# Four copies of the row of k's maxima, and a spread read that takes them by quarters of the partitions

## The chip, the cores and the metric

One core of one Trainium2 chip runs the whole program in one launch. The metric is the device time of an execution in microseconds (us). The engines are TensorE (PE, its weight loads PEld), VectorE (DVE), ScalarE (ACT), GpSimd (POOL) and SyncE (SP), which here issues every transfer.

## What is computed

Eight batches, eight heads, 576 tokens, head size 64: linear attention, then a gated layer with a causal convolution of five taps as gate.

```python
q_s = softmax(q, axis=-1)                 # over the 64 channels of a head
k_s = softmax(k, axis=2)                  # over the 576 tokens
kv = np.einsum('bhsd,bhse->bhde', k_s, v)
x = np.einsum('bhsd,bhde->bhse', q_s, kv) # then heads side by side: (8, 576, 512)
gate = sigmoid(sum(conv_w[t] * x shifted by 4 - t tokens))
out = (gate * (x @ w_val)) @ w_out
```

Softmax over k's tokens needs, for each of the 512 columns (head and channel), the maximum over 576 tokens. This maximum, its way into a tile, is what the change is about.

## The kernel before, in words

Each batch is a unit of work. Its tokens stand in five parts of up to 128 (four full, and a tail of 64 that two batches share); its 512 channels in four blocks of 128. For a batch, TensorE forms kv from the exponentials of k and from v (line 407), turns q (439), multiplies the turned q with kv to x (attend, 487), and makes two products with the weights, value and project (534), each in three passes, since operands are split in a high and a low part. DVE, ACT and POOL do the softmaxes, the convolution (taps: `tap` on DVE, `far` on ACT with `near` on POOL), the splits and the copies out of PSUM.

The order is written out by hand: the list ORDER names every step, and each engine takes its instructions from the list in that order. The engines wait for each other through semaphores alone. SyncE has one queue: a DMA that waits holds back all behind it. Batches are staggered: k of batch 3 is prepared while batch 1 goes through the products.

For batches 2 to 7 the maxima of k go this way:

- `load_km b j` (line 281) loads a copy of k with the channels on partitions: partition p holds the channels 4p to 4p+3, one j at a time. `k_peak b j` (286) reduces it on DVE over the tokens to one column of the tile `kpk`, [128, 4].
- `k_row b` (288 to 291) writes `kpk` to a row of 512 numbers in DRAM, `krow`: 16 bytes from each partition, side by side.
- `k_spread b` (293 to 296) reads this one row of 2 KB into every one of the 128 partitions of the tile `kmax`, [128, 512]. It waits on SyncE until `k_row` has landed. `kmax` has a single buffer, so a batch's spread also waits until the batch before has been subtracted.
- `k_sub b i` (298 to 301) subtracts `kmax` from the five parts of k, most on POOL, some on DVE; `k_exp` and `kt_exp` (305, 309) take exponentials on ACT, and `kv` uses them.

Other steps that are spoken of: `load_q` (209, 211), whose tile `q_max` (361) reduces on DVE; `load_k` (199), 1 MB; `load_kt` (204), the tails of k of two batches; `load_v` (215); `copy b n` (through line 171 on ACT or 173 on DVE) from PSUM into one of the two buffers `o`; and `put b n` (577), the store of such a block to the output. In the list, `k_spread 2` has `put 0 0`, `load_km 3 0` and `load_q 3` after it on SyncE; `k_spread 3` has `put 0 3` right after it.

Of the kernel before, what the change touches and what calls it, by code (L numbers as in the profile page):

```python
# [7 lines left out]
F32 = mybir.dt.float32  # L8
# [9 lines left out]
C = H * D  # L18
P = 128
NB = C // P  # L20
MAIN = 4 * P
TAPS = 5
HALF = S // 2
KM = 3
F32_BATCHES = (0, 1)
EPS = 1e-9
MOST = 122880 - 2.0 ** -7
# [119 lines left out]
def gated_linear_attention(ctx: ExitStack, tc: tile.TileContext, q, k, v, qt, kt, vt, kc, km, w_val, w_out, ident_in, out):  # L147
    nc = tc.nc
# [5 lines left out]
    rowpool = ctx.enter_context(tc.tile_pool(name="rowpool", bufs=1, space=bass.MemoryType.DRAM))  # L154
# [5 lines left out]
    def block(tag, name, bufs, dtype=F32, n=S):  # L160
        return work.tile([P, S], dtype, tag=tag, name=name, bufs=bufs)[:, :n]
# [13 lines left out]
    def times(e, out, in_, factor):  # L175
        if e == "a":
            nc.scalar.mul(out, in_, factor)
        elif e == "p":
            nc.gpsimd.tensor_scalar(out, in_, factor, 1.0, op0=ALU.mult, op1=ALU.mult)
        else:  # L180
            nc.vector.tensor_scalar_mul(out, in_, factor)

    T = {}
# [54 lines left out]
    def part(i, e="a"):  # L238

        lo = T["words", i][:, :, 0].bitcast(U32)  # L240
        f = T["f", i] = block("f", f"f{i}", KM, I32, lo.shape[1])
        times(e, f, lo, 2.0 ** -29)
# [35 lines left out]
    def load_km(b, j):  # L278

        t = T["km", b, j] = block("f", f"km_{b}_{j}", KM)  # L280
        nc.sync.dma_start(out=t, in_=km[b, j])
# [5 lines left out]

    def k_row(b):

        t = T["krow", b] = rowpool.tile([C], F32, tag=f"krow{b}", name=f"krow{b}")  # L290
        nc.sync.dma_start(out=t.rearrange("(p j) -> p j", j=NB), in_=T["kpk", b])

    def k_spread(b):

        t = T["kmax", b] = small.tile([P, C], F32, tag="kmax", name=f"kmax_{b}", bufs=1)
        nc.sync.dma_start(out=t, in_=T["krow", b].rearrange("(o n) -> o n", o=1).broadcast_to([P, C]))

    def k_sub(b, i, e="p", h="a"):
        mx, cs = T["kmax", b], cols(h)
# [141 lines left out]
    def q_across(b):  # L441
        if ("qT", b) not in T:
            T["qT", b] = work.tile([P, NB, S], F32 if b in F32_BATCHES else F32R, tag="qT", name=f"qT_{b}")
        return T["qT", b]
# [31 lines left out]
    def attend(b, p):  # L476

        T["x", b, p] = halved_bank(f"x_{b}_{p}")
        qh = T["qT", b][:, p]
        if b in F32_BATCHES:  # L480
            parts = ((kvd[b % 2][:, p], qh),)
# [161 lines left out]
```

## Time and profile before

| | |
|---|---|
| median of 3 runs | 304.78 us (304.15 to 305.87) |
| the profiled execution | 305.72 us, of which the span is 303.9 |
| k_row (`krow<-kpk`), 6 issues | 2.0 KB each, median 3.5 us from issue to landing |
| k_spread (`kmax<-krow`), 6 issues | 256.0 KB each, median 4.0 us |
| k tails (`kt<-in_k_tail`), 3 issues | 256.0 KB each, median 2.9 us |
| DMA packets of the run | 17454, 51.25 MB |

The span runs from the first to the last instruction; the 1.8 us more of the execution lie around it. In rows of instructions the first number is the start in us from the span's start, the second the duration. In rows of groups the three numbers behind the colon are the shortest, the median and the longest duration in ns. The row "DMA to landing" gives the same three, in us, from a DMA's issue to its landing. A bracket at a row's end tells how long the engine was idle before it, and what ended that.

### The profile page before, as it was taken

To read this page: it belongs to the slowest core of one execution; us is meant where nothing else is said; L and a number is where in the kernel's file an instruction comes from. 1 tells how busy PE (TensorE), PEld (TensorE's weight loads), DVE (VectorE), ACT (ScalarE), POOL (GpSimd) and SP (SyncE) were. 2 spreads that over 40 slices of the span, in tenths; PEclk is the share of its full clock that TensorE was granted. 3 is DMA by queue.
4 is the path that set the end of the run, shared out by engine and by line. 5 is a ranking of instruction groups with operands and counts; after the bars stand their busy time and mean duration, and the time that the engine had idled before them with its cause. 6 is when DMAs were issued, how large, how long until landed. Compare 5 with 4: busy or idle time off the path is not lost.

```text
span 303.9 us, 6467 instructions
## 1 busy us (share of the span) xinstructions
PE 279.1 (92%) x2536; PEld 271.1 (89%) x2536; DVE 255.5 (84%) x350; ACT 216.2 (71%) x357; POOL 220.4 (73%) x206
## 2 busy tenths in 40 slices
PE   0347899999999899999999999999999999999995
PEld 0336699999989799999999999999998999999995
DVE  3999999999999798999999898999779876836611
ACT  3999999967795996869673964659496885464220
POOL 4677959799989699659787879784886949752500
PEclk9978999999999999999999999999999999999999
DMA  7999491389598822618597099023201210021012
GB/s 240 408 405 396 156 397 45 103 187 361 194 319 261 327 102 75 217 54 284 158 395 304 39 259 332 17 90 106 38 0 39 80 41 0 2 116 41 0 62 96
DMA packets 17454, 51.25 MB, mean 169 GB/s; under 512 B 2705, under 2 KB 3089, under 8 KB 14737
## 3 DMA queue, kind: packets, MB, share of 16 engines
q1 hardware_dynamic: 17424, 50.85, 47.9%
q8 instruction: 20, 0.33, 0.5%
q14 instruction: 10, 0.07, 0.1%
HBM read 41.39 MB, written 9.45 MB: 167 GB/s over the span
## 4 chain that ended last, share of the span: by engine, by line
PE 66%; ACT 11%; DVE 10%; DMA 7%; issue 2%; POOL 2%; SPq 1%; ACTq 0%; DVEq 0%
PE out L534 26%; PE val L534 25%; PE x L487 7%; PE kv L407 4%; PE qTps L439 3%; DVE qs L377 3%; DMA q<-in_q 3%; DMA words<-in_w_val 2%; ACT q L392 2%; DMA out<-o 2%; DVE qm L361 1%; ACT L523 1%; DVE qs L378 1%; ACT qT L171 1%; DVE gate L511 1%
## 5 line engine op out<-in xcount | busy, mean ns | idle before, releaser
L534 PE MATMUL val<-x,w_val_hi 128*128 128x288 f32 x512 | 88.4, 294 | 0.0
L534 PEld LDWEIGHTS val<-x,w_val_hi 128*128 128x128 f32 x512 | 74.8, 188 | 0.0
L511 DVE SCALAR_TENSOR_TENSOR gate<-x,cw,gate 128x573 f32<-128x573 f32 (+3 forms) x91 | 72.1, 807 | 2.2 <-ACT gate L500 1.2
L520 POOL TENSOR_TENSOR gate<-gate,far 128x572 f32<-128x572 f32 (+3 forms) x37 | 49.5, 1341 | 27.3 <-ACT far L516 26.4
L534 PE MATMUL out<-gh,w_out_lo 128*128 128x288 f32 x256 | 55.9, 297 | 1.1 <-ACT o L171 0.6
L534 PE MATMUL val<-x,w_val_lo 128*128 128x288 f32 x256 | 56.0, 299 | 0.0
L534 PE MATMUL out<-gh,w_out_hi 128*128 128x288 f32 x256 | 55.0, 294 | 0.0
L534 PEld LDWEIGHTS out<-gh,w_out_lo 128*128 128x128 f32 x256 | 41.2, 188 | 2.1 <-ACT o L171 0.9
L534 PEld LDWEIGHTS val<-x,w_val_lo 128*128 128x128 f32 x256 | 40.7, 188 | 0.7 <-DVE x L173 0.2
L534 PEld LDWEIGHTS out<-gh,w_out_hi 128*128 128x128 f32 x256 | 41.2, 188 | 0.0
L560 POOL TENSOR_TENSOR gl<-g,gh 128x576 fp32r<-128x576 f32 x24 | 34.6, 1449 | 7.2 <-ACT gh L171 5.0
L534 PE MATMUL out<-gl,w_out_hi 128*128 128x288 f32 x256 | 39.2, 294 | 0.0
L516 ACT ACTIVATE far<-x,cw 128x572 f32<-128x572 f32 (+3 forms) x37 | 27.0, 745 | 13.7 <-DVE gate L511 6.7
L534 PEld LDWEIGHTS out<-gl,w_out_hi 128*128 128x128 f32 x256 | 35.7, 188 | 0.0
L552 DVE TENSOR_TENSOR g<-val,gate 128x576 f32<-128x576 f32 x32 | 24.0, 751 | 10.0 <-PE val L534 5.8
L366 POOL TENSOR_TENSOR q<-q,qm 128x512 f32<-128x512 f32 x29 | 31.0, 1086 | 0.7 <-issue 0.7
L171 ACT COPY o<-out 128x576 f32<-128x576 f32 x27 | 17.2, 637 | 16.7 <-PE out L534 11.5
L301 POOL TENSOR_TENSOR k<-k,kmax 128x512 f32<-128x512 f32 x21 | 28.6, 1377 | 0.1
L506 DVE TENSOR_TENSOR x<-x,x 128x576 fp32r<-128x576 f32 x32 | 23.2, 747 | 6.3 <-ACT far L516 4.1
L523 ACT ACTIVATE gate<-gate 128x576 f32<-128x576 f32 x32 | 21.1, 685 | 8.4 <-DVE gate L511 5.4
L394 POOL TENSOR_TENSOR q<-q,qs 128x512 f32<-128x512 f32 x25 | 26.0, 1048 | 0.8 <-DVE qs L379 0.6
L500 ACT ACTIVATE gate<-x,cw 128x576 f32<-128x576 f32 x27 | 19.9, 747 | 6.8 <-PE x L487 5.2
(88 smaller groups left out, 522.1 us busy)
## 6 DMA issues: line engine op xcount, KB each, us to landing
out<-o SPq DMA_DIRECT2D x31, 288.0 KB, 2.2
v<-in_v SPq DMA_DIRECT2D x8, 1040.0 KB, 8.9
q<-in_q SPq DMA_DIRECT2D x7, 1024.0 KB, 7.7
km<-in_k_strided SPq DMA_DIRECT2D x24, 288.0 KB, 4.8
k<-in_k SPq DMA_DIRECT2D x6, 1024.0 KB, 7.9
kc<-in_k_channels SPq DMA_DIRECT2D x8, 288.0 KB, 7.6
words<-in_w_val SPq DMA_DIRECT2D x4, 517.0 KB, 6.9
words<-in_w_out SPq DMA_DIRECT2D x4, 512.0 KB, 7.7
```

The lines of the kernel that those rows point to most:

```text
L301: engine(e).tensor_sub(kk[r, cs], kk[r, cs], mx[r, cs])
L366: engine(e).tensor_tensor(qq, qq, m, op=ALU.add if b < 2 else ALU.subtract)
L394: engine(e).tensor_mul(qq, qq, s.unsqueeze(2).broadcast_to([P, H, D]))
L487: nc.tensor.matmul(T["x", b, p][:, cs], a, z[:, cs], start=(i == 0), stop=(i == len(parts) - 1))
L506: nc.vector.tensor_sub(xl, T["x", b, p], T["xh", b, p].bitcast(F32))
L511: nc.vector.scalar_tensor_tensor(out=a, in0=x, scalar=w, in1=a, op0=ALU.mult, op1=ALU.add)
L516: nc.scalar.activation(T["far", b, p, j], T["x", b, p][:, :S - n], AF.Copy, scale=cw[:, p, j:j + 1])
L520: nc.gpsimd.tensor_add(a, a, T["far", b, p, j])
L523: nc.scalar.activation(T["gate", b, p], T["gate", b, p], AF.Sigmoid)
L534: nc.tensor.matmul(ps[:, cs], a[:, kb, ms], z[:, cs], start=(i == 0), stop=(i == len(parts) - 1))
L552: nc.vector.tensor_mul(T["g", b, m], T["val", b, m], T["gate", b, m])
L560: engine(e).tensor_sub(T["gl", b, m], T["g", b, m], T["gh", b, m].bitcast(F32))
```

## The change

`krow` becomes four times as long: four copies of the row, 2 KB each, one behind the other. `k_row` is still one DMA; its source repeats each partition's four numbers four times, and its destination puts each repeat into another copy. `k_spread` is still one DMA; its source pattern is now 4 copies x 32 repeats x 512 numbers, so that partitions 0 to 31 read the first copy, 32 to 63 the second, and so on. It was 128 repeats x 512 numbers. ORDER, the buffers in SBUF and all other steps are as they were; the number of instructions on each engine and their order are unchanged.

```diff
+ROWS = 4
...
     def k_row(b):
 
-        t = T["krow", b] = rowpool.tile([C], F32, tag=f"krow{b}", name=f"krow{b}")
-        nc.sync.dma_start(out=t.rearrange("(p j) -> p j", j=NB), in_=T["kpk", b])
+        t = T["krow", b] = rowpool.tile([ROWS * C], F32, tag=f"krow{b}", name=f"krow{b}")
+        peaks = T["kpk", b].unsqueeze(1).broadcast_to([P, ROWS, NB])
+        nc.sync.dma_start(out=t.rearrange("(a p j) -> p a j", a=ROWS, j=NB), in_=peaks)
 
     def k_spread(b):
 
         t = T["kmax", b] = small.tile([P, C], F32, tag="kmax", name=f"kmax_{b}", bufs=1)
-        nc.sync.dma_start(out=t, in_=T["krow", b].rearrange("(o n) -> o n", o=1).broadcast_to([P, C]))
+        own = T["krow", b].rearrange("(a n) -> a n", a=ROWS)
+        nc.sync.dma_start(out=t, in_=own.unsqueeze(1).broadcast_to([ROWS, P // ROWS, C]))
```

## The prediction

> **What bounds the kernel now.** I read the page's totals first, then the waits of PE, then the chain of work that ended last.
>
> ```profile
> span 303.9 us, 6467 instructions
> PE 279.1 (92%) x2536; PEld 271.1 (89%) x2536; DVE 255.5 (84%) x350; ACT 216.2 (71%) x357; POOL 220.4 (73%) x206
> ```
>
> TensorE is the bound: 279.1 of 303.9 us, and most of what is left lies ahead of its first matmul. So an edit to two small DMAs matters only where it makes PE wait, or ends one of its few waits. From 30 us on PE's list of waits has six entries, each of a single wait, and none is longer than the first (who waits, for whom: us in total, times, longest):
>
> ```profile
> PE x L487 <- ACT k L171: 0.8, 1, 0.8
> ```
>
> Nothing large can be won; an added wait, on the other hand, is paid in full, since PE has almost no idle time later to give it back from. The question is therefore where the two changed DMAs stand on a chain that reaches PE. The chain of work over 60 to 110 us, in order of time (start, length, what), answers it:
>
> ```profile
> 65.09 8.03 DMA q<-in_q
> ...
> 91.73 5.04 DMA out<-o
> ...
> 104.24 3.44 PE out L534 x24
> ```
>
> Two transfers lie on it: the load of q for batch 3, and the store of one output block (put 0 3), whose buffer the copy of a later block needs. SyncE's queue shows what was issued just ahead of each:
>
> ```profile
> 62.70 0.33 SPq L296 DMA_DIRECT2D kmax<-krow  x1
> ...
> 65.09 0.47 SPq L209 DMA_DIRECT2D q<-in_q  x1
> ...
> 91.28 0.33 SPq L296 DMA_DIRECT2D kmax<-krow  x1
> 91.73 0.34 SPq L577 DMA_DIRECT2D out<-o  x1
> ```
>
> In both places it is k_spread, the very DMA that the change rewrites: for batch 2 shortly ahead of the q load (a store and a km load stand between them), for batch 3 directly ahead of the store. And both landings are waited for without slack (square brackets: idle before, and its releaser), on DVE, on ACT, and through ACT's next pieces on PE (the last row is a window: its length, then the busy us of PE, PEld, DVE, ACT and POOL):
>
> ```profile
> 73.14 2.29 DVE L361 TENSOR_REDUCE qm<-q 128x32 f32<-128x2048 f32 x1 [0.41 <-DMA q<-in_q]
> ```
>
> ```profile
> 96.85 0.64 ACT L171 COPY o<-out 128x576 f32<-128x576 f32 x1 [3.25 <-DMA out<-o]
> ```
>
> ```profile
> 102.72 0.81 PE L487 MATMUL x<-qT,kvs 128*128 128x288 f32 x4 [0.76 <-ACT o L171]
> ```
>
> ```profile
> 96.85:102.70 5.85, 5.11 (x39) 4.88 (x37) 3.92 (x4) 5.77 (x7) 3.85 (x4) 1.00 0.97 385
> ```
>
> From 96.85 to 102.7 ACT is busy for 5.77 of 5.85 us, and PE has already waited 0.76 us there. So a microsecond more on that store is a microsecond of PE.
>
> **The change, part by part.** No instruction moves: every engine's row of instructions is the same before and after, and only the two access patterns differ, six times each.
>
> *k_row* sends 512 pieces of 16 bytes where it sent 128. SyncE waits for it before it can issue k_spread, and everything behind in its queue waits too:
>
> ```profile
> SPq L296 <- DMA krow<-kpk: 17.6, 6, 4.9
> ```
>
> Its price comes from landings. The quickest k_row landed in 1.9 us (first row: minimum, median, maximum), a store of 144 KB takes 1.8 us:
>
> ```profile
> DMA to landing us min/median/max: 1.9/3.9/6.6
> ```
>
> ```profile
> out<-o SPq DMA_DIRECT2D x2, 144.0 KB, 1.8
> ```
>
> So the pieces themselves are about 0.1 us of the 1.9, the rest is fixed. Four times as many make +0.3 us; the lower bound is 0, the upper +1.9, if all of the landing grew by as much again. I take 0.3, from the nearer row, the store.
>
> *Issuing k_spread.* Its pattern gains a step. Six issues took 319 to 327 ns, those of the k load 333 to 1007 ns:
>
> ```profile
> L296 SPq DMA_DIRECT2D kmax<-krow x6: 319/326/327, 62.7 to 212.2; - x6
> ```
>
> ```profile
> L199 SPq DMA_DIRECT2D k<-in_k x6: 333/518/1007, 37.1 to 179.4; - x6
> ```
>
> The bounds are 0 and +0.7 us; I take +0.2, nearest to the k load's median.
>
> *Carrying k_spread* is the large term. The source pattern's outermost step counted 128 (all rows the same row). Now it counts 4, with 32 repeats inside. If the transfer is dealt out over the 16 DMA engines by outermost steps, there are four to deal: four engines with 64 KB each instead of sixteen with 16 KB. No transfer of this trace has fewer than 128 outermost steps, so no row shows such a case, but the price has near rows. A k load of 1024 KB also brings 64 KB to each engine, a kt load of 256 KB 16 KB. Their landings, k's first and then kt's (minimum, median, maximum):
>
> ```profile
> DMA to landing us min/median/max: 5.4/7.9/10.7
> ```
>
> ```profile
> DMA to landing us min/median/max: 2.9/2.9/8.2
> ```
>
> The quickest of each differ by 5.4 - 2.9 = 2.5 us for 48 KB more per engine. Against that stands a gain. Batch 7's spread, with nothing else in flight, took 3.8 us where kt takes 2.9:
>
> ```profile
> kmax<-krow SPq DMA_DIRECT2D x1, 256.0 KB, 3.8
> ```
>
> I read the 0.9 us as the cost of sixteen engines reading one 2 KB row; with one engine to each copy it goes. Net, a spread alone would land 2.5 - 0.9 = 1.6 us later, and four engines are held that much longer. The Trainium skill says the same in "DMA: Bandwidth & Descriptors", "Why a DMA increments its semaphore by 16 and not by 1": the number of engines is the largest up to 16 that divides the slowest step of both patterns; that would be 4 here, and it speaks against the change; no run here shows it yet. The same page's 27 GiB/s per engine makes an estimate of 1.7 us for the 48 KB where the rows give 2.5, and by it the sum below would be +0.5 us.
>
> What of the 1.6 us reaches the two transfers? Later packets on those four engines stand behind the spread, and catch up only in idle time. DMA share is the last but one column:
>
> ```profile
> 63.00:75.00 12.00, 12.00 (x87) 11.47 (x86) 11.38 (x14) 10.12 (x14) 12.00 (x12) 1.00 0.92 308
> 91.00:97.00 6.00, 6.00 (x47) 6.00 (x47) 5.89 (x8) 2.69 (x5) 5.92 (x7) 1.00 0.80 216
> ```
>
> Between the spread and the q load's landing (10 us at 0.92) 0.8 us is idle: 1.6 - 0.8 = 0.8 us later. The issue of that q load hangs on PE, not on k_row, so the first two terms don't add. For the store (6 us at 0.80) 1.2 is idle: 0.4 later, plus 0.3 and 0.2, since it is issued right after k_row's landing and k_spread's issue: 0.9 us.
>
> *Batches 4 to 7* cost nothing. The issues of batches 4 and 5 on SyncE (batch 7's, at 212.2, is the last start in the row of issues above), and the first readers of their tiles, on POOL and for batch 7 on DVE:
>
> ```profile
> 126.13 0.32 SPq L296 DMA_DIRECT2D kmax<-krow  x1
> ...
> 147.29 0.33 SPq L296 DMA_DIRECT2D kmax<-krow  x1
> ```
>
> ```profile
> 130.12 1.30 POOL L301 TENSOR_TENSOR k<-k,kmax 128x512 f32<-128x512 f32 x1
> ...
> 136.46 2.69 POOL L520 TENSOR_TENSOR gate<-gate,far 128x573 f32<-128x573 f32 x2 [3.46 <-ACT far L516]
> ...
> 155.28 1.30 POOL L301 TENSOR_TENSOR k<-k,kmax 128x512 f32<-128x512 f32 x1
> ```
>
> ```profile
> 235.15 0.91 DVE L301 TENSOR_TENSOR k<-k,kmax 128x512 f32<-128x512 f32 x1
> ```
>
> Batch 4's spread is read 4.0 us after its issue. With the three terms it comes 2.1 us later than now and may be a microsecond too late for POOL, which has 3.46 us of idle time soon behind to make it good. In batch 5 the first reader follows 8 us after the issue, in batch 7 23 us; batch 6 lies between. Without that cover each late spread would cost up to its 2.1 us.
>
> **Sum.** 0.8 (batch 2, through q) + 0.9 (batch 3, through the store) = +1.7 us. The two add, as the second follows the first on the same chain. The profiled execution took 305.7 us (303.9 of span); that makes 307.4. It lay 0.9 above the median of 304.78; on the median I forecast 306.5 us.
>
> **Rivals.**
> *Not slower: the transfer stays on 16 engines.* Only k_row's 0.3 and the issue's 0.2 are added, at batch 3. Reading four rows could take back part of the 0.9 us of the spread. That gives between -0.4 and +0.5 us: 304.4 to 305.3. For it: nothing in before shows a transfer on fewer. Against: none of its transfers has so short an outer step. It decides if the spread alone still lands within 3.8 us.
> *Faster by over 0.5%* (1.5 us, about what a measurement of this kernel can tell from no change) would need more than the one store's wait to go; of PE's waits of at most 0.8 us only the one at 102.7 has been traced back here to a DMA. It would give about 303.
> *Much slower: the row stays contended.* Four engines read four neighbouring rows, and the 0.9 us isn't won. Then the spread alone lands 2.5 us later, and of that 1.7 and 1.3 reach the two transfers, or all of it twice if the idle time doesn't help; with 0.5 at batch 3 that is +3.5 to +5.5 us, in the middle +4.5: 309.3. The busiest spread of before (5.9 us) speaks for it:
>
> ```profile
> DMA to landing us min/median/max: 3.1/4.0/5.9
> ```
>
> **Chances.** Few engines as summed 0.55, sixteen engines 0.24, contended 0.18, faster 0.03. The first case runs from +0.5 (idle time covers all but k_row and the issue) to +3.7 (it covers nothing); about six tenths of it, 0.33, are above 1.5 us. So slower 0.33 + 0.18 = 0.51, faster 0.03, the same 0.46. The range leaves out the worse half of the contended case, the lowest part of the sixteen-engine one, and faster: 304.6 to 309.3.
>
> **What would show it.** Right: batch 7's spread lands in about 5.4 us; k_row at its quickest in 2.2; DVE's wait for q at 73 grows by about 0.8, ACT's for the store at 96.8 by 0.9, and PE's at 102.7 follows. Wrong: a lone spread of 3.8 us or less, or one of 5.4 with PE's waits unchanged, which would mean that the two transfers do not queue behind it.

## The result and the profile after

The changed kernel took 309.54 us (median of 4 runs, 308.96 to 309.96) against 305.32 us before (4 runs): ratio 1.0138, 95% interval 1.0093 to 1.0184. It was measured twice more, beside more runs of before: 307.51 against 305.17 (ratio 1.0073, 1.0046 to 1.0100) and 307.70 against 305.35 (1.0078, 1.0045 to 1.0112). So it is slower by some 2.3 us in two measurements and by 4.2 us in the first; the intervals (1.4 to 3.4 us, and 2.8 to 5.6) overlap. The profiled execution of the first measurement took 309.16 us, of which the span is 307.3. In the table of experiments below, the medians of e1, e13 and e14 count one slow run each (469 to 708 us) that their ratios leave out.

First the question on which the large term rested: on how many DMA engines does the spread run? A transfer closes with a small completion packet on every engine that carried a part of it; the windows below show 16 of them, then 4. The hardware queue of before, then of after (packets, MB, share of 16 engines):

```profile
q1 hardware_dynamic: 17424, 50.85, 47.9%
```

```profile
q1 hardware_dynamic: 19656, 50.88, 47.6%
```

These are 2232 packets more. k_row alone should add 6 x 384 = 2304, one for each further piece of 16 bytes. The 72 that are missing are 6 x 12: each spread ends with 4 completions instead of 16. Batch 7's spread, alone in the queue, shows the engines themselves. Windows around it of before (212 to 217 us), of after (216 to 221 us), each with the busy share of the 16 engines in tenths and GB/s in 40 slices; the packets under 512 B are its completions:

```profile
DMA  0000000000009249968998884452000000000000
GB/s 0 0 0 0 0 0 0 0 0 0 0 0 98 16 33 115 197 197 164 213 164 147 164 164 66 147 180 99 0 0 0 0 0 0 0 0 0 0 0 0
DMA packets 145, 0.27 MB, mean 54 GB/s; under 512 B 16, under 2 KB 16, under 8 KB 144
```

```profile
DMA  0000000000002212222512212222222221000002
GB/s 0 0 0 0 0 0 0 0 0 0 0 0 49 66 66 115 98 98 98 98 66 98 82 66 82 98 98 98 98 115 115 82 115 66 16 33 16 33 16 82
DMA packets 133, 0.27 MB, mean 54 GB/s; under 512 B 4, under 2 KB 4, under 8 KB 132
...
q14 instruction: 1, 0.01, 0.4%
```

The busy share falls from eight or nine tenths to two (4 of 16 is 0.25), and the rate from about 160 to about 95 GB/s. All four completions lie within the second window; what its last slice shows is in part a packet of another queue (the row q14). So the spread's traffic ends 4.7 us after its issue (216.25), where before it ended 3.3 us after (212.23): about 1.5 us later.

Where does this reach PE? In PE's list of waits, x behind a copy by ACT now has two entries; before it had one.

```profile
PE x L490 <- ACT o L172: 2.4, 2, 1.4
```

ACT's copy that waits for put 0 3, and PE behind it, in the changed kernel:

```profile
98.97 0.64 ACT L172 COPY o<-out 128x576 f32<-128x576 f32 x1 [5.14 <-DMA out<-o]
```

```profile
99.67 0.80 PE L490 MATMUL x<-qT,kvs 128*128 128x288 f32 x4 [1.45 <-ACT o L172]
...
104.84 0.81 PE L490 MATMUL x<-qT,kvs 128*128 128x288 f32 x4 [0.94 <-ACT o L172]
```

The copy starts 2.1 us later than before (98.97 against 96.85), and so does PE's second step (104.84 against 102.72). SyncE's rows tell why:

```profile
86.16 0.38 SPq L293 DMA_DIRECT2D krow<-kpk  x1
...
91.97 0.55 SPq L299 DMA_DIRECT2D kmax<-krow  x1
92.64 0.39 SPq L580 DMA_DIRECT2D out<-o  x1
```

The store goes out at 92.64 instead of 91.73, 0.9 us later. Of this, 0.2 us is k_row's own later issue (86.16 against 85.94), 0.5 its longer landing, and 0.2 the longer issue of k_spread. The store then takes 6.26 us in the chain of work where it took 5.04, behind a spread on four engines:

```profile
92.64 6.26 DMA out<-o
```

So far PE has lost 2.1 of the 3.4 us by which the span has grown. Part of the rest is lost at a place of which the prediction said that it costs nothing. POOL, then PE, at batch 4:

```profile
133.58 1.30 POOL L304 TENSOR_TENSOR k<-k,kmax 128x512 f32<-128x512 f32 x1 [1.29 <-DMA kmax<-krow]
134.84 0.90 POOL L477 TENSOR_TENSOR qTlo<-qTt,qT 128x128 fp32r<-128x128 f32 x1
```

```profile
135.26 0.29 PE L490 MATMUL x<-qTlo,kvs 128*128 128x288 f32 x1
135.79 0.40 PE L490 MATMUL x<-qTlo,kvs 128*128 128x288 f32 x1 [0.24 <-POOL qTlo L477]
136.03 0.43 PE L537 MATMUL out<-gh,w_out_lo 128*128 128x288 f32 x2
```

The same work of PE before, the two multiplications with qTlo in one row:

```profile
133.22 0.43 PE L487 MATMUL x<-qTlo,kvs 128*128 128x288 f32 x2
133.49 0.43 PE L534 MATMUL out<-gh,w_out_lo 128*128 128x288 f32 x2
```

The instruction right behind the waiting k_sub on POOL, tail_low, makes an operand of PE's next step. POOL's idle time, at 136 us in the profile before, was to make the wait good; it comes behind this instruction, too late. The wait of 0.24 us is only what PE still shows of it: PE reaches the first of the two multiplications 2.0 us behind the profile before (135.26 against 133.22), and the product after them 2.5 us behind (136.03 against 133.49). At batch 5 the same order of steps costs another 0.4 us or so. There k_sub waits for a late load of k, and tail_low again stands behind it:

```profile
159.78 1.30 POOL L304 TENSOR_TENSOR k<-k,kmax 128x512 f32<-128x512 f32 x1 [1.93 <-DMA k<-in_k]
161.05 0.46 POOL L477 TENSOR_TENSOR qTlo<-qTt,qT 128x128 fp32r<-128x128 f32 x1
```

The last 0.4 us are lost in smaller steps after that and have not been traced.

### The profile page after: what moved, and what is told of

It reads as the page before. It is cut to its first block, busy times and chain, and to the rows that moved or that the text cites. A ratio compares the mean times of both kernels' runs of the same rounds, so it can differ in the third digit from the quotient of the medians.

```text
span 307.3 us, 6467 instructions
## 1 busy us (share of the span) xinstructions
PE 280.9 (91%) x2536; PEld 271.8 (88%) x2536; DVE 255.3 (83%) x350; ACT 216.2 (70%) x357; POOL 221.4 (72%) x206
## 4 chain that ended last, share of the span: by engine, by line
PE 51%; DVE 14%; ACT 14%; DMA 13%; issue 3%; POOL 2%; SPq 1%; ACTq 0%; POOLq 0%; DVEq 0%
PE out L537 23%; PE val L537 19%; PE x L490 5%; DMA out<-o 4%; DVE qs L380 4%; PE kv L410 3%; DVE gate L514 2%; DMA k<-in_k 2%; DMA words<-in_w_val 2%; DMA krow<-kpk 2%; ACT q L395 2%; DVE qm L364 2%; PE qTps L442 2%; ACT L526 2%; DMA kmax<-krow 2%
```

## The experiments

Each ratio is that of the kernel to the one before, with its 95% interval, from runs on the same chip. It is not the quotient of the two medians; differences in us below are those of the medians, unless an interval stands with them, and the two can differ by some tenths.

| kernel | median us | before us | ratio (95%) |
|---|---|---|---|
| e1 copies only | 305.91 | 305.39 | 1.0013 (0.9994 to 1.0032) |
| e2 copies, sixteen engines | 305.72 | 305.39 | 1.0012 (0.9994 to 1.0030) |
| e3 two copies | 316.59 | 305.39 | 1.0362 (1.0321 to 1.0404) |
| e4 batch 3 only | 306.85 | 305.39 | 1.0048 (1.0032 to 1.0064) |
| e5 all but batch 3 | 305.89 | 305.23 | 1.0013 (0.9990 to 1.0036) |
| e6 stores early | 309.75 | 305.23 | 1.0151 (1.0120 to 1.0182) |
| e7 before, stores early | 306.50 | 305.23 | 1.0044 (1.0028 to 1.0060) |
| e9 POOL's order | 307.33 | 305.23 | 1.0064 (1.0041 to 1.0086) |
| e10 batches 2 and 3 | 306.61 | 304.94 | 1.0053 (1.0033 to 1.0072) |
| e11 batches 3 to 7 | 307.61 | 304.94 | 1.0080 (1.0056 to 1.0104) |
| e12 loads later | 307.59 | 304.94 | 1.0086 (1.0053 to 1.0119) |
| e13 before, loads later | 305.91 | 304.94 | 1.0023 (1.0003 to 1.0043) |
| e14 before, loads last | 304.22 | 305.17 | 0.9964 (0.9944 to 0.9984) |
| e15 both covers | 305.06 | 305.17 | 1.0005 (0.9987 to 1.0022) |
| e16 the change again | 307.51 | 305.17 | 1.0073 (1.0046 to 1.0100) |
| e17 batches 4 to 7 | 305.99 | 305.17 | 1.0031 (1.0007 to 1.0055) |
| e18 the change, third time | 307.70 | 305.35 | 1.0078 (1.0045 to 1.0112) |
| e19 loads last again | 303.64 | 305.35 | 0.9952 (0.9937 to 0.9968) |

**The parts of the change: e1, e2, e3.** Against the changed kernel:

```diff
e1, k_spread:
-        nc.sync.dma_start(out=t, in_=own.unsqueeze(1).broadcast_to([ROWS, P // ROWS, C]))
+        nc.sync.dma_start(out=t, in_=own[0:1].broadcast_to([P, C]))
e2, k_spread:
+        nc.sync.dma_start(out=t, in_=own.unsqueeze(0).broadcast_to([P // ROWS, ROWS, C]))
e3:
-ROWS = 4
+ROWS = 2
```

> k_row writes four copies as in the changed kernel, but k_spread reads the first copy with the pattern of before (128 repeats of one row). Four-engine theory (the spread holds four DMA engines four times as long, and the transfers behind it are late): the spread lands as before, only k_row's extra 384 pieces are left, +0.1 to +0.5 us over before. Rival, k_row (four times the small writes hold SyncE's queue): most of the +4 us stays, +2.5 us or more.

> k_row writes four copies; k_spread reads them with 32 repeats outermost and the 4 copies inside, so neighbouring partitions read different copies and the outermost step counts 32. Four-engine theory: sixteen engines again, 16 completions per spread in the packet count instead of 4, the time within 0.7 us of before (k_row's 0.2, the longer issue's 0.2). If one row read by all engines is slow, as I read the 3.8 against 2.9 us, the lone spread of batch 7 lands in about 3.0 us and the time may fall by up to 0.4 us. Rival (k_row or the longer issue): +2.5 us or more.

> Two copies instead of four: 256 pieces in k_row, the spread's outermost step counts 2. Four-engine theory: two engines with 128 KB each, 28 completions fewer per two spreads (2 per spread instead of 16), the lone spread of batch 7 has its last packet 5.4 us after its first (3.4 with four), and the time goes up by 5 to 15 us over the changed kernel. Rival (k_row's pieces): half of them are gone, so it is faster than the changed kernel, about +2 us over before.

By their ratios, e1 and e2 are both 0.4 us over before, each with an interval from 0.2 below zero to 1.0 or less. With the four copies written and read, but on sixteen engines, little is left of the loss, so neither k_row's 512 pieces nor the longer issue (e2's takes nearly as long as the change's) is the main cause. In e2 the hardware queue has 19728 packets, 2304 more than before, so no completion is missing. The first row is e2's spread of batch 7 alone, with its landing; the second is its six issues:

```profile
kmax<-krow SPq DMA_DIRECT2D x1, 256.0 KB, 2.9
```

```profile
L299 SPq DMA_DIRECT2D kmax<-krow x6: 524/524/594, 62.7 to 213.9; - x6
```

e3 writes half the pieces and is 11.2 us slower than before. Its lone spread (window 224.1 to 232.5 us) runs at a busy share of one tenth, at about 50 GB/s, with two completions:

```profile
DMA  0000000111002111111111111111111000040000
...
DMA packets 132, 0.29 MB, mean 34 GB/s; under 512 B 2, under 2 KB 2, under 8 KB 130
```

So the outermost step of the source, 4 or 2, is the number of engines, and that is where the cost comes from. This is the rule of the Trainium skill, "DMA: Bandwidth & Descriptors", section "Why a DMA increments its semaphore by 16 and not by 1"; the runs agree with it at 2 and 4, and at 32 (e2), where all sixteen complete.

**Which batches: e4, e5, e10, e11, e17.** Both edits are made for some batches, the others stay as before. The diff is e4's; where it has b == 3, e5 has b != 3, e10 b in (2, 3), e11 b > 2 and e17 b > 3. In the branch stand the lines of before, and k_spread has the same branch:

```diff
 def k_row(b):
+        if not (b == 3):
...
+            return
```

> Both edits for batch 3 alone, the other batches as before. Theory of the one store: PE loses about 2 us at 97 to 103 us and nothing elsewhere, +1.8 to +2.3 us over before. Rival, each batch pays alike: a sixth of the 4 us, +0.7 us.

> Both edits for batches 2 and 4 to 7, batch 3 as before. If the batches' losses add, 4.2 less the 1.5 of batch 3 alone: +2.3 to +2.8 us over before, most of it after 130 us. Rival, batch 3's store is all that counts: within 0.6 us of before.

> Both edits for batches 2 and 3. Batch 3 alone cost 1.5 us and all the others together 0.4, but all six 4.2, so some loss arises from two together. If batch 2's late start feeds batch 3 (DVE later, so k_row 3 later, so the store later): +2.3 to +3.2 us. If not: +1.3 to +1.8.

> Both edits for batches 3 to 7, batch 2 as before. If batch 3's lateness is what makes batches 4 and 5 lose (their own late spreads and loads then meet POOL later in its order): +2.8 to +4.2 us. If batch 2 is needed for the loss beyond 1.9 us: +1.5 to +2.2.

> Both edits for batches 4 to 7 alone. If these batches lose only when batch 3 is late: +0.0 to +0.5 us. If they lose by themselves what batches 3 to 7 lost over batch 3 alone (2.7 less 1.5): +1.0 to +1.4 us.

Batch 3 alone costs 1.5 us, under the 1.8 to 2.3 that the theory of the one store gave; with batch 2 besides 1.7, batches 4 to 7 alone 0.8, batches 3 to 7 2.7. That batch 2 adds anything is not shown. 1.5 + 0.8 = 2.3 is what the second and the third measurement of the whole change gave. The results of e11 and e17 lie between the two ranges that each was expected to decide, so they do not tell whether a late batch 3 makes batches 4 to 7 lose more. e5, with batches 2 and 4 to 7, gave 0.4 by its ratio (0.3 below zero to 1.1), less than e17's 0.9 (0.2 to 1.7), but the intervals overlap. e17's profile has the same two rows as the changed kernel, here without any help from batch 3, on POOL and on PE:

```profile
132.06 1.30 POOL L312 TENSOR_TENSOR k<-k,kmax 128x512 f32<-128x512 f32 x1 [1.78 <-DMA kmax<-krow]
```

```profile
134.27 0.41 PE L498 MATMUL x<-qTlo,kvs 128*128 128x288 f32 x1 [0.72 <-POOL qTlo L485]
```

**Taking the store out of the way: e6, e7.** Two stores go ahead of k_row 3, in the changed kernel (e6) and in the one before (e7). Here and below, a diff of the list shows only the steps that move:

```diff
-    k_row 3,
...
-    k_spread 3,
...
-    put 0 3,
...
-    put 0 2,
...
+    put 0 2, put 0 3, k_row 3,
...
+    k_spread 3,
```

> The changed kernel with put 0 2 and put 0 3 issued ahead of k_row 3, so that neither the wait for k_row 3, nor the longer issue, nor the spread on four engines stands ahead of them; nothing else is moved. If batch 3's loss is those stores' late landing, it goes, and with it the 0.76 us that PE waited at 102.7 us before the change: 2 to 3 us faster than the changed kernel, +1.2 to +2.2 over before. Rival, batch 3's loss comes through the tile that the spread fills (POOL waited 2.2 us for it): no more than 0.5 us faster than the changed kernel.

> The kernel before with the same two stores moved, no other edit. If PE's 0.76 us wait at 102.7 us hangs on the store behind the spread, it goes: -0.5 to -1.2 us. Rival: that wait only changes its releaser: within 0.3 us of before.

Neither gained: e6 is no faster than the change, as its rival had it, and e7 is 1.3 us slower than before, which neither of its two cases allowed. ACT's copy at 95 us no longer waits for a store, but now k_row 3 stands in the DMA queue behind 576 KB of stores, and in e7 k_spread 3 is issued at 94.0 instead of 91.3 us. In e7, SyncE, POOL, ACT and PE:

```profile
85.75 0.33 SPq L291 DMA_DIRECT2D krow<-kpk  x1
...
94.01 0.32 SPq L296 DMA_DIRECT2D kmax<-krow  x1
```

```profile
98.93 1.29 POOL L301 TENSOR_TENSOR kt<-kt,kmax 64x512 f32<-64x512 f32 x1 [2.86 <-DMA kmax<-krow]
```

```profile
100.25 0.63 ACT L309 ACTIVATE ktz<-kt 64x512 f32<-64x512 f32 x1 [1.71 <-POOL kt L301]
```

```profile
104.82 0.85 PE L534 MATMUL out<-gh,w_out_lo 128*128 128x288 f32 x2 [1.53 <-ACT far L516]
```

The tile that the spread fills is a second path from batch 3 to PE, through POOL's k_sub and ACT's kt_exp and far, only a little shorter than the store's. Lifting one transfer over another in this full queue swapped the paths.

**POOL's order: e9.** In the changed kernel, tail_low goes ahead of the k_sub that may wait:

```diff
-    k_sub 4 1 p, tail_low 3 1 p,
+    tail_low 3 1 p, k_sub 4 1 p,
...
-    k_sub 5 1 p, q_low 4 0, tail_low 4 0 p, g_high 3 2 a, k_sub 5 2 p, q_low 4 1, attend 4 1, tail_low 4 1 p,
+    q_low 4 0, tail_low 4 0 p, g_high 3 2 a, q_low 4 1, attend 4 1, tail_low 4 1 p, k_sub 5 1 p, k_sub 5 2 p,
```

> The changed kernel with three steps of POOL's order changed: tail_low 3 1 ahead of k_sub 4 1, and tail_low 4 0 and 4 1 ahead of k_sub 5 1 and 5 2, so that POOL makes what PE needs before it waits for a late spread or a late load of k. If batches 4 and 5 lose through that order, PE's steps at 135 and 161 us go: 0.6 to 1.0 us faster than the changed kernel. Rival, the loss there is DMA load in general: no difference over 0.3 us.

It is 2.2 us faster than the changed kernel's first measurement, but only 0.2 to 0.4 us faster than the other two. Its profile has no wait of PE for qTlo from POOL, so that wait is gone; what this is worth by itself is not shown.

**An empty queue for batch 3: e12 to e15, e19.** The 1 MB loads of v and k for batch 4, which stand before and behind k_row 3, are not needed for 40 us. They go after put 1 1 (e12 in the changed kernel, e13 in the one before; the first added line), or after load_kt 4 (e14 and e19 in the one before; e15 in the changed kernel, with e9's order on POOL; the second added line, in place of the first):

```diff
-    load_v 4,
...
-    load_k 4,
...
+    put 1 1, load_v 4, load_k 4,
...
+    load_kt 4, load_v 4, load_k 4,
```

> The changed kernel with the 1 MB loads of v and k for batch 4 issued after put 1 1 instead of around k_row 3, so that k_row 3, the spread and the two stores behind it meet an empty queue. If batch 3's loss is queueing of these small transfers among large ones: k_row 3 lands in about 3 us instead of 5.8, ACT's wait for the store at 99 us is down from 5.1 to under 2 us, and the time is 2 to 3 us less than the changed kernel's. Rival, four engines are slow enough by themselves: under 1 us less.

> The kernel before with the same two loads moved, no other edit. If the wait at 102.7 us is the same queueing: 0.5 to 1.2 us faster than before. Otherwise within 0.3 us of before.

> The kernel before with the loads of v and k for batch 4 issued after load_kt 4, so that no km load stands behind them (in the run with the loads after put 1 1, DVE waited 2.06 us for one). If the 0.76 us wait of before was a loss: 0.8 to 1.8 us faster than before. If PE's head start is bounded by POOL or DVE later anyway: within 0.4 us of before.

> The changed kernel with the same two loads moved and with POOL's order as in the run of that name; spreads on four engines as before. If the store of batch 3 and POOL's order at batches 4 and 5 are the whole path: within 0.7 us of before or faster. If four engines cost by themselves: +1.5 us or more over before.

> The kernel before with the loads of v and k for batch 4 after load_kt 4, a second time: 0.6 to 1.4 us faster than before, if the first measurement holds; within 0.3 us of before if it was chance.

e12 gained at batch 3 (k_row 3 landed in about 3 us, and ACT's wait for the store fell from 5.14 to 2.38 us), and in e13 PE's wait at 102.7 us was gone. But both gave it back: e12 took the time of the later measurements of the change, and e13 was 0.7 us slower than before by its ratio. A km load now stood behind the moved ones, and DVE waited for it in e13:

```profile
113.70 0.75 DVE L286 TENSOR_REDUCE kpk<-km 128x1 f32<-128x576 f32 x1 [2.06 <-DMA km<-in_k_strided]
```

With the loads one place further back that wait is gone. By their ratios e14 is 1.1 us faster than before, and e19, the same kernel measured again, 1.5 us: both intervals exclude no change. In e14, k_row 3 lands in under 2.5 us, the store is out 2.1 us earlier, and ACT waits for PE, no longer for a store:

```profile
86.71 0.33 SPq L291 DMA_DIRECT2D krow<-kpk  x1
89.20 0.33 SPq L296 DMA_DIRECT2D kmax<-krow  x1
89.62 0.38 SPq L577 DMA_DIRECT2D out<-o  x1
```

```profile
95.66 0.64 ACT L171 COPY o<-out 128x576 f32<-128x576 f32 x1 [1.25 <-PE out L534]
```

e15 has the spreads on four engines still, and takes the time of before, 2.45 us less than e16, measured with it. So most of the loss came through the store of batch 3 and through the order behind the late tiles. But the moved loads gain about 1.1 us without the change as well (e14, measured with e15), and e15 is still 0.8 us slower than e14 by the medians and 1.3 by the ratios, whose intervals do not meet. So four engines are not free even here. In e15's profile POOL waits 0.94 us for the spread of batch 4, and at 136.8 us PE waits 0.34 us for ACT's far, which e14's does not; that the one leads to the other is not shown. The kernel before with both moves was not measured.

**The change again: e16, e18.**

> The changed kernel itself in the same call as its parts. If the parts add up with what batch 3's lateness does to batches 4 to 7: +2.6 to +3.4 us, so that the first 4.2 was at the upper end of its interval. If there is a further loss from batch 2: +4 us or more.

> The changed kernel a third time. If its cost is batch 3's 1.5 and batches 4 to 7's 0.8: +2.0 to +2.8 us. If the first call was the rule: +3.7 us or more.

The results are +2.3 and +2.35 us, less than e16 was expected to give and inside e18's first range. The profiles of the three measurements differ in when the store of batch 3 is in. ACT's copy behind it started at 98.97 in the first, here in e16, and in e18:

```profile
97.40 0.64 ACT L172 COPY o<-out 128x576 f32<-128x576 f32 x1 [3.75 <-DMA out<-o]
```

```profile
98.29 0.64 ACT L172 COPY o<-out 128x576 f32<-128x576 f32 x1 [4.84 <-DMA out<-o]
```

Between the first and the second lie 1.6 us, with the same program. Most of this lies ahead of the spread, in k_row 3. From its issue to that of the spread it took 5.8 us in the first (5.3 before), and 4.4 here in e16:

```profile
85.94 0.38 SPq L293 DMA_DIRECT2D krow<-kpk  x1
...
90.34 0.55 SPq L299 DMA_DIRECT2D kmax<-krow  x1
91.01 0.40 SPq L580 DMA_DIRECT2D out<-o  x1
```

In e18 it took 5.5. From the store's issue to ACT's copy, on the other hand, the three took 6.3 to 6.4 us each, and before 5.1. So the store behind the spread is 1.2 us slower than before each time, and k_row's landing decides how much of it shows. In e1 and e2, which have the long k_row but the spread on sixteen engines, the store took 3.9 us: the delay is that of the four engines. Why k_row landed later in the first measurement is not settled. PE's step that stood at 102.72 before starts at 104.84, 103.27 and 104.16, and the spans are longer by 3.4, 1.5 and 1.8 us: how the loss is split between batch 3 and what follows also varies from profile to profile.

## Why the prediction was right or wrong

The direction and the main mechanism were right: four engines, and a store behind them that is waited for. Two steps failed: that idle time of the DMA engines takes back 1.2 of the spread's 1.6 us ahead of the store, and that batches 4 to 7 cost nothing. The forecast was +1.7 us, with a range up to 309.3; the first measurement, 309.54, lay above it, the later two (+2.3 us) inside. Step by step:

- *k_row, +0.3.* Too small as a landing: the quickest went from 1.9 to 2.8 us (row below, of after). As a cost of the whole it was about right: e1, which has this edit alone, measured +0.4 us, with an interval from 0.2 below zero to 1.0 above. At batch 3, where the sum needs it, k_row's time differs by more than this between profiles of one program (4.4 to 5.8 us).

```profile
DMA to landing us min/median/max: 2.8/3.5/4.4
```

- *The issue, +0.2.* Right: 537 to 668 ns against 319 to 327.

```profile
L299 SPq DMA_DIRECT2D kmax<-krow x6: 537/539/668, 62.8 to 216.3; - x6
```

- *Four engines, a lone spread 1.6 us later.* Shown, by completions and busy share, and by e3 at two. The profile gives no landing for a spread on four engines, so the forecast of 5.4 us can't be read off; its traffic ended about 1.5 us later after its issue than before, which fits.
- *The 0.9 us that sixteen engines lose on one row.* Not borne out in this size. e1 reads one row with sixteen engines, and its lone spread took 3.0 us, hardly more than e2's 2.9 from four rows:

```profile
kmax<-krow SPq DMA_DIRECT2D x1, 256.0 KB, 3.0
```

In e7, e13, e14 and e19, which read one row as before does, the lone spread took 3.1 to 3.6 us. The 3.8 us of before were one draw; I had made a property of a single row of the trace. Against the spread of e1, whose traffic ended 2.7 us after its issue, that of the changed kernel ended 2.0 us later; that the net 1.6 fits the one profile of before is in part luck.
- *Batch 2, +0.8 through the q load.* DVE's q_max did start 0.9 us later (74.06 against 73.14), but its row shows no wait for the load any more. The chain of work of after goes through put 0 0 instead, the store right behind the spread, and through ACT's copy behind it: the same path as at batch 3, which the prediction passed over here. Little of it reached PE, as the path had slack after all. The chain of work, of before and then of after, shows where part of it was made good: a pass of DVE over the sums, L378 before and L381 after, took 0.7 us less and ended at 80.2 and 80.4 us; what it waits for inside is not shown. e10 less e4 gives 0.2 us, too little to tell from nothing.

```profile
63.85 5.82 DMA out<-o
```

```profile
74.06 2.28 DVE L364 TENSOR_REDUCE qm<-q 128x32 f32<-128x2048 f32 x1
```

```profile
78.86 1.32 DVE qs L378
```

```profile
79.76 0.63 DVE qs L381
```

- *Batch 3, +0.9 through the store.* The right place, sized too low: e4 measured 1.5 us (1.0 to 2.0). The term at fault is the 0.4 us, that is, the idle 1.2 us that was to be taken off 1.6: the store itself was 1.2 us slower than before in all three profiles. A mean busy share of 0.80 over sixteen engines did not tell how much idle time the four engines had when the store needed them.
- *"Batches 4 to 7 cost nothing."* This step failed: e17 measured 0.8 us (0.2 to 1.7). POOL's late k_sub was seen, and that POOL has idle time behind it; that the very next instruction on POOL feeds PE was overlooked.

The two errors at batches 2 and 4 (0.6 too much, 0.8 too little) nearly cancel, which is luck, and batch 3's 0.6 remains: 1.7 against 2.3 us. The sixteen-engine rival falls with the engine count. The contended one, with +4.5, was near the first measurement in its number, but not in its mechanism: e1 and e2 show no loss of 0.9 us on one row that could be left over.

## What to carry to other kernels

When a transfer is rearranged, look at the outermost step of both of its patterns: here the count there became the number of DMA engines, and a pattern with the copies inside and the repeats outside (e2) kept all sixteen. Price a late tile not at its first reader but at what stands behind that reader on its engine. Do not take a mean busy share of all DMA engines as room for a transfer that waits behind few of them. Compare a remedy with the kernel that has the same remedy and not the change (e15 with e14, not with before). And ask of large loads whether they are due: moving two 1 MB loads out of the way of three small transfers gained 1.1 and 1.5 us (e14, e19), while four copies read by sixteen engines (e2) gained nothing.

## What was not expected of the hardware

Lifting a transfer to the front of a queue cost more than it gained, since a tiny DMA behind it (k_row 3, 2 KB) landed later, the more bytes stood ahead of it. From its issue to that of k_spread it took 8.3 us in e7, behind a 1 MB load and two stores, 5.3 us before, behind the load alone, and 2.5 us in e14, without either. The number of pieces mattered for the tiny one: in five profiles with 128 pieces of 16 bytes the quickest landed in 1.5 to 2.1 us, in nine with 512 in 2.4 to 3.0. And the same program took 309.5 us in one measurement and 307.5 to 307.7 in two others, while the kernel before stayed at 304.9 to 305.4; why it varies more is not settled.
